# Ten pairs instead of eight beside the preparation of the weights, and the experts two pairs later

## The chip, the core and the metric

The kernel runs on one core of one Trainium2 chip. The metric is the device time of one execution in microseconds (us), the median of several runs. The engines are named as the profile names them: PE is the matrix engine (PEld its loading of weights), DVE the vector engine, ACT the scalar engine that does tanh and exp, POOL the general engine, and SP the engine whose queue issues most of the DMAs. Each engine and each queue works its instructions off in order.

## The reference

Three layers follow each other. B = 4 batches, S = 448 positions, all in float32.

```python
# attention, 12 heads of 64
scores = cap * tanh((q @ k.T) / sqrt(64) / cap)
x = softmax(scores) @ v                        # (4, 448, 768)
# four experts, each a causal attention with one head of 64; a position takes its best two
logits = x @ w_gate
for e in range(4):
    a = causal_softmax((x @ wq[e]) @ (x @ wk[e]).T / sqrt(64))
    out += gate[e] * (a @ (x @ wv[e]) @ wo[e])
# MLP with a gate over the positions
h = gelu(out @ w_in); u, v = halves of h
y = out + (u * (w_sg @ layernorm(v) + b_sg)) @ w_out
```

## The kernel before

**Pairs.** The attention is worked off in 24 pairs of heads, six (HP) for each batch. `slot(i, side)` writes out the program of pair i: the scores of its first half and their tanh and exp on ACT (p), the weighted sum of the values of pair i-1 (po), the scores of the second half, the sums of the exps of every second pair (sum), and the adding up of the exps on DVE (pb; from the second batch on POOL does a part of it). At five places it calls `side(place)`, which puts other work there: "a" twice, beside the halves of the scores, then "w", "p" and "n". Instructions keep this order on PE, DVE, ACT and POOL until the attention ends; after it a planner that simulates the time orders them by itself.

**Preparation.** Beside the first eight pairs (PRE_SLOTS = HP + 2, lines 613 and 625) the side work is `prepare_weights`. The first MLP weight (w_in, stored in 64-bit words) comes in 12 units: `convert(u)` turns one into float32 with seven DVE instructions, `products(u)` multiplies it with wo (PE, w2ps) and at the end of each half `rnd`/`rest` split the product into a high part on ACT and a low part on DVE (w2h, w2l). `turns`, `u_loads` and the expression in line 601 say at which pair a unit is converted, loaded and multiplied. `split_x(k)` splits the experts' weights wqk and wvg, one of six blocks of rows in each of the pairs 2 to 7 (loads by `load_x`).

**Normalising a batch.** After the sixth pair of a batch the sums are inverted on DVE, written to DRAM (rd) and read back over all partitions (rb, `load_rb`); `over_sums` multiplies the attention's output (os) by them and `in_parts` splits it into xh and xl, the experts' inputs. `normed(n, place)` says where: loads at pair 0 of the next batch, place "n"; two products and the first split at pair 1, "n"; the rest within pair 2.

**Experts.** `PLAN` spreads the experts' work of a batch over eleven steps. `planned(n)` (line 491) puts step 0 of batch b at pair 6(b+1)+2: queries and keys (qk, steps 0, 1, 4, 5), values (v, steps 2, 3), scores (a) with their exps (pe) (`weigh`, steps 2, 3, 6, 7), transposes (tr, `turn`) and the weighted values (av, `attend`). What is left after pair 24 comes from `experts_end`, beside the MLP (`mlp_a`, `mlp_b`, `mlp_c`: hv, hu, sp, o).

**Other side work.** `w_out` converts the MLP's last weight in eight pieces through the buffers rb0 and rb1, which `load_rb` uses too: a load (wuw), DVE instructions (wum), three on POOL, and two stores to DRAM (wud). From pair 8 on it takes three pieces in six pairs (lines 518 to 522).

Of the kernel before, what the change touches and what calls it, by code (L numbers as in the profile page):

```python
# [10 lines left out]
F32 = mybir.dt.float32  # L11
# [10 lines left out]
B, H, S, D = 4, 12, 448, 64  # L22
HP = H // 2
DM = H * D
KC = DM // 128
E, HD = 4, 64
# [11 lines left out]
def drain(gen):  # L38
    for _ in gen:
        pass  # L40
# [16 lines left out]
def together(main, side, ratio):  # L57

    yield from interleave(main, side, ratio)
    yield from side  # L60
# [12 lines left out]
def build(ctx: ExitStack, tc: tile.TileContext, a: dict):  # L73
    nc = tc.nc
# [3 lines left out]
    def rnd(eng, out, in_):  # L78

        if eng == "a":  # L80
            act.activation(out, in_, AF.Copy)
        elif eng == "v":
            dve.tensor_copy(out, in_)
        else:
            pool_e.tensor_scalar(out, in_, 1.0, 0.0, op0=ALU.mult, op1=ALU.add)

    def rest(eng, out, in_, hi):

        e = dve if eng == "v" else pool_e
        e.tensor_tensor(out, in_, hi.bitcast(F32), op=ALU.subtract)  # L90
# [127 lines left out]
    def values(b, hp, vv):  # L218
        po = ps_o.tile([128, 512], F32, tag="po", name=f"po{b}_{hp}")
        for c in range(NC):  # L220
            for j in range(2):
                mm(po[64 * j:64 * j + 64, :S], vv[:, j, c, :], pend[b, hp][c // 2][:, j, c % 2, :],
                                 start=(c == 0), stop=(c == NC - 1))
            yield 805.0
        if hp % 2 == 0:
            os_t[b, hp // 2] = ao.tile([128, 2, S], F32, tag="os", name=f"os{b}_{hp}", bufs=4)
        act.activation(os_t[b, hp // 2][:, hp % 2, :], po[:, :S], AF.Copy)

    def sums(b, i):
# [19 lines left out]
    def slot(i, side):  # L249

        if i == 0:
            ld[0] = load_pair(*pairs[0])
            ld[1] = load_pair(*pairs[1])
        if i + 2 < len(pairs):
            qk = [at.tile([128, S], F32, tag=t, name=f"{t}{i + 2}", bufs=3) for t in ("qp", "kp")]
            b, hp = pairs[i + 2]
            nc.sync.dma_start(qk[1], a["kT"][b, :, hp, :])
            nc.sync.dma_start(qk[0], a["qT"][b, :, hp, :])  # L260
            ld[i + 2] = qk
        if i < len(pairs):
            first = scores(*pairs[i], 0, *ld[i][:2])
            drain(islice(first, 2))
            side("a")
            drain(first)
        side("w")
        if i:
            b, hp = pairs[i - 1]
            drain(values(b, hp, ld.pop(i - 1)[2]))  # L270
        if 0 < i < len(pairs) - 1:
            b, hp = pairs[i + 1]
            vv = at.tile([CP, 2, NC, D], F32, tag="vv", name=f"vv{b}_{hp}", bufs=3)
            nc.sync.dma_start(vv, a["v"][b, :, 2 * hp:2 * hp + 2])
            ld[i + 1] = (*ld[i + 1], vv)
        if i < len(pairs):
            side("a")
            drain(scores(*pairs[i], 1, *ld[i][:2]))
        side("p")
        if i:  # L280
            b, hp = pairs[i - 1]
            if hp % 2 == 1:
                drain(sums(b, hp // 2))
        if i < len(pairs):
            add_up(*pairs[i])
        side("n")
# [6 lines left out]
    def load_rb(b, h2):  # L293
        rb = rbs[b, h2] = xp.tile([128, 2, S], F32, tag=f"rb{h2 % 2}", name=f"rb{b}_{h2}")
        for r in range(2):
            nc.sync.dma_start(rb[64 * r:64 * r + 64],
                              rb_d[b][r::2, h2:h2 + 1, :].rearrange("r o s -> o r s").to_broadcast([64, 2, S]))

    def over_sums(b, h2):
        x = os_t[b, h2]  # L300
        dve.tensor_mul(x, x, rbs.pop((b, h2)))
        if h2 == 0:
            load_rb(b, 2)

    def in_parts(b, h2):

# [7 lines left out]
    def normed(n, place):  # L314

        b = (n - 1) // HP - 1
        step = (n % HP, place)
        if n > B * HP + 2:
            return
        if step == (0, "n"):  # L320
            load_rb(n // HP - 1, 0)
            load_rb(n // HP - 1, 1)
        elif b < 0:
            return
        elif step == (1, "n"):
            over_sums(b, 0)
            over_sums(b, 1)
            in_parts(b, 0)
        elif step == (2, "a0"):
            in_parts(b, 1)  # L330
        elif step == (2, "w"):
            over_sums(b, 2)
        elif step == (2, "a1"):
            in_parts(b, 2)

    wu_done = []
# [150 lines left out]
    def planned(n):  # L487

        work = {"a": [], "w": [], "p": [], "t": [], "n": []}
        for b in reversed(range(B)):  # L490
            for place, f, *args in PLAN.get(n - (b + 1) * HP - 2, []):
                work[place].append((b, f, args))
        return work

    def run(works):
        for b, f, args in works:
            w = f(b, *args)
            if w is not None:
                yield from w

    ws = [w_out(k, i) for k in range(4) for i in range(2)]

    def beside(n):

        work = planned(n)
        halves = ["a0", "a1"]

        def side(place):
            if place == "a":
                drain(run(work["a"][:1]))  # L510
                del work["a"][:1]
                normed(n, halves.pop(0))
            elif place == "p":
                drain(together(run(work["p"]), run(work["t"]), 0.3))
            else:
                drain(run(work[place]))
                normed(n, place)
            if place == "n" and n > HP + 1:
                if n % HP in (3, 4, 5) and ws:
                    drain(ws.pop(0))  # L520
                if n % HP in (2, 3, 4) and ws:
                    next(ws[0])
        return side

    def experts_end(n):

        for m in range(n, B * HP + 20):
            work = planned(m)
            for place in ("a0", "w", "a1", "n"):
                normed(m, place)  # L530
            for place in "aw":
                yield from run(work[place])
            yield from together(run(work["p"]), run(work["t"]), 0.3)
            yield from run(work["n"])
            if ws:
                yield from ws.pop(0)


    def prepare_weights(pool):
# [7 lines left out]
            raw[u] = pool.tile([128, FH], I64, name=f"wi{n}_{k}w", tag="w64", bufs=5)  # L547
            nc.sync.dma_start(raw[u], a["w_in"][:, k, n * FH:(n + 1) * FH])

        def load_x(k):  # L550
            for name, w in (("wqk", 2 * E * HD), ("wvg", E * HD + E)):
                t = st[name, k] = pool.tile([128, w], F32, tag=f"st{name}", name=f"{name}{k}", bufs=2)
                nc.sync.dma_start(t, a[name][:, k, :])

        def convert(u):
            m = pool.tile([128, FH], I32, name=f"wi{u}m", tag="m64", bufs=5)
            e = pool.tile([128, FH], I32, name=f"wi{u}e", tag="e64", bufs=2)
            p, e = from64(raw.pop(u), m, e)
            dve.tensor_tensor(p, p, e, op=ALU.add)
            parts[u] = p  # L560

        def split_x(k):
            for name, hi, lo in (("wqk", wqk_h, wqk_l), ("wvg", wvg_h, wvg_l)):
                t = st.pop((name, k))
                rnd("a", hi[:, k, :], t)
                rest("v", lo[:, k, :], t, hi[:, k, :])

        def products(u):
            n, k = units[u]
# [10 lines left out]
                    for o, d in ((oh, w2_d[0]), (ol, w2_d[1])):  # L580
                        nc.sync.dma_start(d[:, m, n * 512:(n + 1) * 512], o.bitcast(F32))

        turns = [(0,), (1, 2), (3, 4), (5, 6), (7, 8), (9, 10), (11,), ()]
        u_loads = [(1, 2, 3), (4, 5), (6, 7), (8, 9), (10, 11), (), (), ()]

        def side(n):
            todo = list(turns[n])

            def at_place(place):
                if place == "a" and todo:  # L590
                    convert(todo.pop(0))
                elif place == "w":
                    for u in u_loads[n]:
                        load(u)
                    if n == 0:
                        nc.sync.dma_start(wt, a["woT"])
                        st["neg"] = constants(pool)
                    if 0 < n <= KC:
                        load_x(n - 1)
                elif place == "p" and n > 1:  # L600
                    for u in (2 * n - 4, 2 * n - 3):
                        products(u)
                elif place == "n":
                    if n == 3:
                        dve.tensor_copy(neg[:, S - CP:], st.pop("neg"))
                    if n > 1:
                        split_x(n - 2)
                if n > 0:
                    normed(n, place)
            return at_place  # L610
        return load, side

    PRE_SLOTS = HP + 2

    xp = ES(tc.tile_pool(name="xp", bufs=1, reuse_waits="tile"))
    with tc.tile_pool(name="pre", bufs=2) as pre:
# [85 lines left out]
    st = {}  # L702
# [184 lines left out]
```

## Time and profile before

| what | value |
|---|---|
| median of 3 runs | 584.55 us (582.46 to 584.84) |
| the profiled execution | 582.48 us, span 580.7 us |
| busy share of the span | PE 93%, DVE 63%, ACT 56%, POOL 25% |
[...]
| DMA | 53.98 MB, mean 93 GB/s |
| chain that ended last | PE 56%, DVE 24%, ACT 8%, DMA 7% of the span |

The span runs from the first to the last instruction; the 1.8 us that the execution takes beyond it lie around it. A share of busy time is a mean over stages with different limits: the chain, which goes back from the last instruction to whatever released each step, has 24% on DVE although PE is busy 93% of the time.

### The profile page before, as it was taken

The page shows a single profiled execution, that of the slowest core. Times are in us where ns is not written, and L with a number is a line of the kernel's source. Part 1 is how long each engine was busy: PE and PEld are TensorE (multiplying, and loading weights), DVE is VectorE, ACT ScalarE, POOL GpSimd, SP SyncE. Part 2 cuts the span into 40 slices and gives each one's busy share as a digit, 9 for nine tenths or more (in the row PEclk, how much of TensorE's full clock was granted, in tenths as well). Part 3 has the DMA queues.
Part 4 walks back from the last instruction along what each step waited for, and adds up shares of the span by engine and source line. Part 5 has one row for each costly group of instructions (what it writes and reads, how often), then busy time and mean ns, then how long its engine had stood idle before and what let it go on. Part 6 is the DMA issues. An engine that isn't in the chain of part 4 may idle for free.

```text
span 580.7 us, 7591 instructions
## 1 busy us (share of the span) xinstructions
PE 540.2 (93%) x2732; PEld 348.1 (60%) x2732; DVE 364.6 (63%) x731; ACT 324.3 (56%) x514; POOL 142.6 (25%) x180
## 2 busy tenths in 40 slices
PE   7999787799899989999989969999999998999997
PEld 2333222455555554554555546778768887989996
DVE  3999997445658456767455469578770589375310
ACT  5988668277777856666857223463553344243211
POOL 0000111033351163431163205327322212031000
PEclk9999999699999999999999986999999999999999
DMA  8966427323326133154011044010601000001111
GB/s 248 333 212 193 135 75 209 97 78 116 108 75 185 50 103 97 35 145 136 17 55 56 28 109 156 21 44 0 216 34 49 16 1 31 33 16 49 49 47 63
DMA packets 28900, 53.98 MB, mean 93 GB/s; under 512 B 3968, under 2 KB 20672, under 8 KB 28864
## 3 DMA queue, kind: packets, MB, share of 16 engines
q1 hardware_dynamic: 27712, 48.26, 27.1%
q0 software_dynamic: 1152, 5.24, 2.5%
q8 instruction: 21, 0.34, 0.3%
q14 instruction: 15, 0.12, 0.1%
HBM read 41.83 MB, written 11.67 MB: 92 GB/s over the span
## 4 chain that ended last, share of the span: by engine, by line
PE 56%; DVE 24%; ACT 8%; DMA 7%; issue 3%; SPq 1%; POOL 1%; DVEq 0%; ACTq 0%; POOLq 0%
PE o L119 15%; PE sp L119 7%; PE qk L119 6%; PE v L119 5%; DVE pb L104 5%; DMA rb<-rd 5%; ACT p L104 5%; PE po L119 4%; PE s L119 4%; PE hu L119 3%; DVE wum L104 3%; PE tr L454 3%; ACT pe L104 2%; PE hv L119 2%; PE a L119 2%
## 5 line engine op out<-in xcount | busy, mean ns | idle before, releaser
L104 ACT ACTIVATE p<-s,tsc 112x896 f32<-112x896 f32 x96 | 91.5, 1007 | 31.4 <-PE s L119 31.4
L119 PE MATMUL s<-qp,kp 64*112 64x448 f32 x384 | 87.6, 557 | 3.9 <-ACT p L104 3.9
L104 ACT ACTIVATE p<-p,capt 112x1792 f32<-112x1792 f32 x48 | 85.9, 1790 | 1.3
L104 POOL TENSOR_TENSOR pb<-p 112x896 f32<-112x896 f32 x18 | 40.2, 2235 | 162.6 <-ACT p L104 155.3
L119 PE MATMUL po<-p,vv 112*64 112x448 f32 x384 | 77.3, 545 | 0.0
L104 DVE TENSOR_TENSOR pb<-pb,p 112x896 f32<-112x896 f32 x48 | 52.1, 1085 | 18.1 <-ACT p L104 17.3
L119 PEld LDWEIGHTS s<-qp,kp 64*112 64x112 f32 x384 | 32.2, 172 | 50.3 <-issue 22.4
L104 ACT ACTIVATE pe<-a,m 112x112 f32<-112x112 f32 (+3 forms) x64 | 31.2, 493 | 51.0 <-DVE m L104 49.6
L119 PE MATMUL qk<-xh,wqk_h 128*128 128x448 f32 x96 | 41.2, 430 | 13.2 <-DVE xh L104 13.2
L119 PEld LDWEIGHTS po<-p,vv 112*64 112x64 f32 x384 | 25.6, 137 | 44.1 <-issue 42.5
L104 POOL TENSOR_SCALAR pe<-pe,cs 112x112 f32<-112x112 f32 (+1 forms) x64 | 35.7, 576 | 50.2 <-DVE cs L104 50.2
L104 DVE CUSTOM_DVE_ANT_0 a<-a,neg 112x112 f32<-112x112 f32 (+3 forms) x64 | 28.0, 464 | 21.3 <-PE a L119 21.2
L119 PE MATMUL a<-qk 64*112 64x224 f32 (+3 forms) x128 | 34.6, 451 | 6.1 <-ACT pe L104 5.8
L119 PE MATMUL qk<-xh,wqk_l 128*128 128x448 f32 x96 | 37.4, 390 | 0.0
L119 PEld LDWEIGHTS qk<-xh,wqk_h 128*128 128x128 f32 x96 | 19.5, 203 | 26.8 <-DVE xh L104 12.5
L119 PE MATMUL o<-gl,wu_h 128*128 128x448 f32 x96 | 35.4, 369 | 0.0
L119 PE MATMUL o<-gh,wu_h 128*128 128x448 f32 x96 | 35.2, 367 | 0.0
L119 PE MATMUL o<-gh,wu_l 128*128 128x448 f32 x96 | 35.0, 368 | 0.0
L104 ACT ACTIVATE ob<-o 128x448 f32<-128x448 f32 x24 | 13.0, 541 | 37.5 <-PE o L119 37.5
L119 PE MATMUL v<-wvg_h,xh 128*112 128x260 f32 x96 | 28.8, 300 | 0.9 <-ACT pe L104 0.9
L119 PEld LDWEIGHTS a<-qk 64*112 64x112 f32 x128 | 13.5, 179 | 26.9 <-ACT pe L104 12.3
L104 DVE COPY pt<-tr 112x112 f32<-112x112 f32 (+3 forms) x32 | 14.0, 448 | 23.9 <-PE tr L454 23.9
(226 smaller groups left out, 1133.6 us busy)
## 6 DMA issues: line engine op xcount, KB each, us to landing
kp<-in_kT_dram SPq DMA_DIRECT2D x24, 224.0 KB, 4.1
qp<-in_qT_dram SPq DMA_DIRECT2D x24, 224.0 KB, 4.2
vv<-in_v_dram SPq DMA_DIRECT2D x24, 224.0 KB, 4.1
rb<-rd SPq DMA_DIRECT2D x24, 224.0 KB, 4.8
out_dram<-ob SPq DMA_DIRECT2D x24, 224.0 KB, 1.9
wuw<-in_w_out_dram SPq DMA_DIRECT2D x8, 384.0 KB, 3.4
wud<-wuw SPq DMA_DIRECT2D x16, 192.0 KB, 1.9
wqk<-in_wqk_dram SPq DMA_DIRECT2D x6, 256.0 KB, 2.9
```

The source lines that it names most:

```text
L104: ins = f(*args, **kw)
L119: pin(nc.tensor.matmul(*args, **kw))
L454: pin(nc.tensor.transpose(g[:CP, j * CP:(j + 1) * CP], pe[:, j * CP:(j + 1) * CP], ident))
```

## The change

The first stage takes ten pairs instead of eight (PRE_SLOTS = HP + 4): `turns`, `u_loads` and the new `u_products` spread the twelve units over them. `load_x` and `split_x` go. `experts_weights(n, place)` takes their place: six parts, cut by columns for wqk (queries and keys of two experts each) and by rows for wvg, loaded at pairs 7 to 12 and split at pairs 8 to 13, the later four beside the experts. The experts' step 0 moves from pair 6(b+1)+2 to pair 6(b+1)+4. `normed` makes two products at pair 2 of the next batch, the third product and the first split at pair 3, the other splits at pair 4; the load of the third rb moves behind both products. The attention's outputs have five buffers instead of four. `slot` calls `side("a")` twice after the last pair too. `w_out` takes two pieces in six pairs, so that two of the eight are left for `experts_end`.

```diff
-            os_t[b, hp // 2] = ao.tile([128, 2, S], F32, tag="os", name=f"os{b}_{hp}", bufs=4)
+            os_t[b, hp // 2] = ao.tile([128, 2, S], F32, tag="os", name=f"os{b}_{hp}", bufs=5)
@@ normed
-        elif step == (1, "n"):
-            over_sums(b, 0)
-            over_sums(b, 1)
+        elif step == (2, "n"):
+            for h2 in range(2):
+                over_sums(b, h2)
+            load_rb(b, 2)
+        elif step == (3, "n"):
             in_parts(b, 0)
-        elif step == (2, "a0"):
+            over_sums(b, 2)
+        elif step == (4, "a0"):
             in_parts(b, 1)
-        elif step == (2, "w"):
-            over_sums(b, 2)
-        elif step == (2, "a1"):
+        elif step == (4, "a1"):
             in_parts(b, 2)
@@ planned
-            for place, f, *args in PLAN.get(n - (b + 1) * HP - 2, []):
+            for place, f, *args in PLAN.get(n - (b + 1) * HP - 4, []):
@@ new
+    def experts_weights(n, place):
+        qk, vg = (wqk_h, wqk_l, a["wqk"]), (wvg_h, wvg_l, a["wvg"])
+        parts = {8: (*qk, 0, KC, 0, 128), 9: (*qk, 0, KC, 256, 384), 10: (*vg, 0, 3, 0, E * HD + E),
+                 11: (*vg, 3, KC, 0, E * HD + E), 12: (*qk, 0, KC, 128, 256), 13: (*qk, 0, KC, 384, 512)}
+        if place == "w" and n + 1 in parts:
+            _, _, d, k0, k1, c0, c1 = parts[n + 1]
+            t = w_raw[n + 1] = at.tile([128, 780], F32, tag="ws", name=f"ws{n}", bufs=2)
...
+            nc.sync.dma_start(t, d[:, k0:k1, c0:c1])
...
+        elif place == "n" and n in parts:
...
+            rnd("a", hi[:, k0:k1, c0:c1], t)
+            rest("v", lo[:, k0:k1, c0:c1], t, hi[:, k0:k1, c0:c1])
@@ beside
-                if n % HP in (3, 4, 5) and ws:
+                if n % HP in (4, 5) and ws:
                     drain(ws.pop(0))
-                if n % HP in (2, 3, 4) and ws:
+                if n % HP in (3, 4) and ws:
                     next(ws[0])
@@ prepare_weights
-        turns = [(0,), (1, 2), (3, 4), (5, 6), (7, 8), (9, 10), (11,), ()]
-        u_loads = [(1, 2, 3), (4, 5), (6, 7), (8, 9), (10, 11), (), (), ()]
+        turns = [(0,), (1,), (2,), (3, 4), (5,), (6, 7), (8,), (9, 10), (11,), ()]
+        u_loads = [(1, 2), (3,), (4, 5), (6, 7), (8,), (9, 10), (11,), (), (), ()]
+        u_products = [(), (), (0,), (1, 2), (3,), (4, 5), (6,), (7, 8), (9,), (10, 11)]
-    PRE_SLOTS = HP + 2
+    PRE_SLOTS = HP + 4
```

## Rows read from the trace of the kernel before

**Rows 1.** Busy time by stretches: us, five engines, granted clock, DMA share, GB/s.
```profile
6.00:90.00 84.00, 75.89 (x316) 26.78 (x316) 77.72 (x123) 67.95 (x69) 4.89 (x2) 1.00 0.63 199
90.00:112.00 22.00, 14.13 (x54) 7.32 (x56) 12.59 (x16) 9.60 (x11) 2.08 (x1) 0.77 0.69 191
325.00:360.00 35.00, 29.46 (x126) 19.62 (x125) 22.29 (x43) 11.34 (x32) 8.59 (x15) 0.80 0.33 89
```

**Rows 2.** Waits of PE up to 112 us: waited for, us in total, times, longest.
```profile
PE qk L119 <- DVE xh L104: 7.9, 3, 4.2
PE w2ps L119 <- DVE w2l L104: 3.0, 1, 3.0
PE s L119 <- ACT p L104: 3.0, 3, 1.7
```

**Rows 3.** A stretch of 4 us, columns as in rows 1.
```profile
348.00:352.00 4.00, 4.00 (x9) 1.79 (x8) 3.05 (x7) 1.26 (x4) 0.00 (x0) 0.50 0.14 21
```

**Rows 4.** The chain of waits, pair 0: start us, us, what.
```profile
6.48 0.96 PE s L119 x4
```

**Rows 5.** Timeline of PE, pair 6 and pair 8's start: start us, us, what.
```profile
67.19 3.23 PE L119 MATMUL po<-p,vv 112*64 112x448 f32 x16
...
70.35 1.76 PE L119 MATMUL s<-qp,kp 64*112 64x448 f32 x8
...
72.04 1.98 PE L119 MATMUL w2ps<-wi8m,wt 128*128 128x512 f32 x4
...
75.67 0.95 PE L119 MATMUL sum<-pb,onehot 112*32 112x448 f32 x4
...
89.81 1.76 PE L119 MATMUL s<-qp,kp 64*112 64x448 f32 x8
```

**Rows 6.** Timeline of PE, pair 9 and pair 10's start.
```profile
112.50 1.76 PE L119 MATMUL s<-qp,kp 64*112 64x448 f32 x8
...
119.04 0.47 PE L119 MATMUL qk<-xh,wqk_h 128*128 128x448 f32 x1
...
122.88 1.76 PE L119 MATMUL s<-qp,kp 64*112 64x448 f32 x8
```

**Rows 7.** Groups of DVE, 6 to 94 us: busy us, mean ns, idle before.
```profile
L104 DVE TENSOR_TENSOR pb<-pb,p 112x896 f32<-112x896 f32 x16 | 17.4, 1084 | 1.7 <-ACT p L104 1.4
...
L104 DVE TENSOR_TENSOR wqk_l<-wqk,wqk_h 128x512 fp32r<-128x512 f32 x6 | 4.1, 685 | 0.0
```

**Rows 8.** Timeline of DVE and POOL, pairs 5 to 7.
```profile
65.93 0.42 DVE L104 TENSOR_SCALAR wi9m<-wi_3w 128x512 int32<-128x512 int32 x1
66.39 0.89 DVE L104 TENSOR_SCALAR wi9m<-wi9m 128x512 f32<-128x512 f32 x2
...
69.83 1.08 DVE L104 TENSOR_TENSOR pb<-p 112x896 f32<-112x896 f32 x1
...
70.38 2.82 POOL L104 TENSOR_TENSOR pb<-p 112x896 f32<-112x896 f32 x1 [68.70 <-ACT p L104]
...
71.29 2.65 DVE L104 TENSOR_SCALAR wi10m<-wi10m 128x512 f32<-128x512 f32 x2
...
93.93 0.42 DVE L104 TENSOR_TENSOR wvg_l<-wvg,wvg_h 128x260 fp32r<-128x260 f32 x1
```

**Rows 9.** Waits of PE from 112 to 325 us.
```profile
PE a L119 <- ACT pe L104: 5.8, 5, 2.4
```

**Rows 10.** Timeline after the last pair, last batch's normalising.
```profile
330.76 0.96 PE L119 MATMUL sum<-pb,onehot 112*32 112x448 f32 x8
...
345.12 0.71 PE L119 MATMUL qk<-xh,wqk_h 128*128 128x448 f32 x1 [4.12 <-DVE xh L104]
...
353.58 1.08 DVE L104 TENSOR_TENSOR xl<-os,xh 128x896 fp32r<-128x896 f32 x1
```

**Rows 11.** Timeline of SP's queue, one piece of w_out.
```profile
299.53 0.33 SPq L344 DMA_DIRECT2D wuw<-in_w_out_dram  x1
310.17 2.47 SPq L351 DMA_DIRECT2D wud<-wuw  x2
```

More of the change, by code (lines that the diff above doesn't have):

```diff
@@ L266, in slot @@
             drain(first)
+        else:
+            side("a")
         side("w")
@@ L275, in slot @@
             ld[i + 1] = (*ld[i + 1], vv)
+        side("a")
         if i < len(pairs):
-            side("a")
             drain(scores(*pairs[i], 1, *ld[i][:2]))
@@ L301, in over_sums @@
         dve.tensor_mul(x, x, rbs.pop((b, h2)))
-        if h2 == 0:
-            load_rb(b, 2)
     def in_parts(b, h2):
@@ L317, in normed @@
         step = (n % HP, place)
-        if n > B * HP + 2:
+        if n > B * HP + 4:
             return
         if step == (0, "n"):
-            load_rb(n // HP - 1, 0)
-            load_rb(n // HP - 1, 1)
+            for h2 in range(2):
+                load_rb(n // HP - 1, h2)
         elif b < 0:
             return
-        elif step == (1, "n"):
-            over_sums(b, 0)
-            over_sums(b, 1)
+        elif step == (2, "n"):
+            for h2 in range(2):
+                over_sums(b, h2)
+            load_rb(b, 2)
+        elif step == (3, "n"):
             in_parts(b, 0)
-        elif step == (2, "a0"):
+            over_sums(b, 2)
+        elif step == (4, "a0"):
             in_parts(b, 1)
-        elif step == (2, "w"):
-            over_sums(b, 2)
-        elif step == (2, "a1"):
+        elif step == (4, "a1"):
             in_parts(b, 2)
@@ L499, in run @@
                 yield from w
+    w_raw = {}
+    def experts_weights(n, place):
[5 more added lines that the diff above has]
+            t = w_raw[n + 1] = at.tile([128, 780], F32, tag="ws", name=f"ws{n}", bufs=2)
+            t = t[:, :(k1 - k0) * (c1 - c0)].rearrange("p (k c) -> p k c", k=k1 - k0)
+            nc.sync.dma_start(t, d[:, k0:k1, c0:c1])
+            w_raw[n + 1] = t
+        elif place == "n" and n in parts:
+            hi, lo, _, k0, k1, c0, c1 = parts[n]
+            t = w_raw.pop(n)
+            rnd("a", hi[:, k0:k1, c0:c1], t)
+            rest("v", lo[:, k0:k1, c0:c1], t, hi[:, k0:k1, c0:c1])
     ws = [w_out(k, i) for k in range(4) for i in range(2)]
@@ L517, in side @@
                 normed(n, place)
+                experts_weights(n, place)
             if place == "n" and n > HP + 1:
-                if n % HP in (3, 4, 5) and ws:
+                if n % HP in (4, 5) and ws:
                     drain(ws.pop(0))
-                if n % HP in (2, 3, 4) and ws:
+                if n % HP in (3, 4) and ws:
                     next(ws[0])
@@ L528, in experts_end @@
             work = planned(m)
-            for place in ("a0", "w", "a1", "n"):
-                normed(m, place)
+            normed(m, "a0")
             for place in "aw":
                 yield from run(work[place])
+            normed(m, "a1")
             yield from together(run(work["p"]), run(work["t"]), 0.3)
             yield from run(work["n"])
+            normed(m, "n")
             if ws:
@@ L548, in load @@
             nc.sync.dma_start(raw[u], a["w_in"][:, k, n * FH:(n + 1) * FH])
[L550 to L553, printed above, removed]
         def convert(u):
@@ L560, in convert @@
             parts[u] = p
[L562 to L566, printed above, removed]
         def products(u):
@@ L597, in at_place @@
                         st["neg"] = constants(pool)
[L598 to L601, printed above, removed]
+                    experts_weights(n, place)
+                elif place == "p":
+                    for u in u_products[n]:
                         products(u)
@@ L605, in at_place @@
                         dve.tensor_copy(neg[:, S - CP:], st.pop("neg"))
-                    if n > 1:
-                        split_x(n - 2)
+                    experts_weights(n, place)
                 if n > 0:
```

## The prediction

> **What bounds the kernel now.** Read first the busy time by stretches [rows 1]. From 6 to 90 us, the pairs 0 to 7, DVE is busy 77.7 of 84 us and PE 75.9, part of it on weights that wait for DVE: here DVE sets the pace. From 90 to 112 us PE stands for 7.9 of 22 us, and from 325 to 360 us for 5.5 of 35; in both the mean granted clock falls, to 0.77 and 0.80. Then the waits of PE [rows 2] name the first of these: 7.9 us for xh, in three waits, the inputs of batch 0's experts. Everywhere else PE has work.
>
> [...]
>
> So the kernel is a sum of PE's work, plus what PE stands and runs slowly in three places: the preparation, the entry of batch 0 into the experts, and that of batch 3.
>
> **The change part by part.** PE's work stays the same, instruction for instruction. What changes is its order.
>
> *First stage and first entry.* Half of a pair's scores costs 72.04 - 70.35 = 1.69 us of PE, the values 70.35 - 67.19 = 3.16, so a pair 6.54; the sums of two pairs 0.95; two units of products 75.67 - 72.04 = 3.63 [rows 5]; one step of queries and keys 122.88 - 119.04 = 3.84 [rows 6]. At 112.50 us [rows 6] PE has pairs 0 to 8 and one such step behind it. After the change it stands at the same step when pair 10 is done, two pairs further: 2 x 6.54 + 0.95 = 14.0 us of work ahead. If pair 9 ends at T, pair 10 ends at T + 6.54 + 3.84 + 0.95 = T + 11.3, and the gain is 14.0 - (T + 11.3 - 112.5) = 115.2 - T.
>
> What is T? By PE: nine pairs without pair 0's values (55.7), ten units (18.2), four sums (3.8), from 6.48 us [rows 4], with the 3.0 us of early waits for ACT [rows 2], bring it to pair 9 at 87.2; pair 9 with two units takes 10.2, so T = 97.4. By DVE: it closes pair 7 at 94.35 [rows 8], when PE had begun pair 8 at 89.81 [rows 5], 4.5 us before. Up to pair 8's adding up the new order has six splits less (6 x (0.685 + 0.42) = 6.6 [rows 7, 8]), the two splits of the second half's product later (1.4, of the same shape as wqk_l's [rows 7]) and one pair's two addings more (2.2 [rows 7]): 88.5 instead of 94.35, with PE again up to 4.5 ahead. So DVE no longer binds on the whole, but it does in single pairs: a conversion takes 69.83 - 65.93 = 3.9 us [rows 8], so pairs 3 and 5 with two of them need 3 x 1.08 + 7.8 = 11.0 on DVE, pair 5 another 1.4, against 10.2 on PE: 3 us together. T = 100, gain 15.2. The low end of T is PE's 97.4 (gain 17.8). The high end is that all ten pairs keep the old pace of (89.81 - 6.48) / 8 = 10.4 [rows 4, 5]: T = 110.6, gain 4.6.
>
> One thing speaks against so early a T. While POOL adds up (70.38, 2.82 us), a pair of DVE instructions that otherwise takes 0.89 takes 2.65 [rows 8]. POOL adds in the pairs from 6 on; there one conversion is left now (unit 11), afterwards four (units 8 to 11, in three pairs). One to three such blocks of 1.76, instead of one, put 0 to 3.5 us on DVE; I take none, as PE's bound lies above. [...]
>
> The wait for xh goes because the sums' way through DRAM (rd, rb) gets two pairs more, some 20 us, before the first product needs it, and the splits another. Next late is then nothing on DVE but PE itself. If that cover failed, the 7.9 us [rows 2] would come back at pair 10 and leave a gain of 7.3, which the range of T still holds.
>
> *Parts of wqk and wvg split beside the experts.* Four of six, each 768 or 780 columns: on DVE about 0.685 x 1.5 = 1.0 us [rows 7], on ACT an estimate of as much. Each is needed one pair later at the earliest. PE has other work beside; the cost is 0 to 4, I take 1. Their loads, 384 KB each on SP's queue between two pairs' loads, are one in a pair, as many bytes as before in fewer DMAs: nothing.
>
> *The weighing of batch 2.* PE waits 5.8 us in five waits for the experts' exps while ACT serves the attention too [rows 9], the longest 2.4. Steps 2 and 3 of batch 2 now fall on pair 24, which has no scores, and behind it: 2 us gained (0 to 2.4).
>
> *The entry of batch 3.* From the last sums (330.76) to the first xh on PE (345.12) are 14.4 us, to the last xl 353.58 + 1.08 are 23.9 [rows 10]. What PE had beside it was one step with transposes. Now steps 3, 4 and 5 of batch 2 stand there: two value chunks and scores of some 6 us (estimated from one qk step plus half), and two steps of 3.84 with transposes of about 1, in all 15 to 16 us. That covers the first xh. It doesn't cover everything: two w_out pieces now come here, through rb0 and rb1, and a piece takes 299.53 to 310.17 + 2.47, and its landing, about 15 us [rows 11]; if one gets rb0 before the third rb, the last xh comes 15 us later, at some 39. Until then PE also has batch 2's steps 6 to 10 (7 us), two thirds of the first qk step (2.6), and the MLP's first part as soon as its weights are there. The standing and slow time of this place is 5.5 + 6 = 11.5 us; the gain lies between all of it and a loss of as much again as the standing (-5.5). I take 5: PE stands once more, shorter.
>
> *The rest costs nothing*: fewer w_out pieces beside the pairs take DVE work away there; the fifth os buffer and the second "a" after the last pair move no instruction onto PE's path.
>
> Sum: 15.2 - 1 + 2 + 5 = 21. Against the profiled execution's 582.48 this gives 561.5; the median of the runs lies 2.1 higher, at 584.55, which gives 563.5. I say 563.
>
> **The rivals.**
> *Only the first half holds:* batch 3's entry stays as dear, because w_out's piece holds the third rb. For it: the buffers are shared, 15 us a piece [rows 11]. Against: 15 us more PE work beside it. 15.2 - 1 + 2 = 16 are left, less up to 2 lost at the end: 569 to 571.
> *It gains everything:* T = 97.4, no cost in the splits, all 11.5 at the end: 17.8 + 2.4 + 11.5 = 32, so 553.
> *The first stage doesn't do what it says:* the blocks by POOL and the alternating pairs keep DVE the limit at 10.4 a pair, gain 4.6 there and 0 at the end: 579.
> *Slower:* both w_out pieces get rb0 before the third rb. The last xh then comes 24 + 30 = 54 us behind the last sums, against some 16 + 7 + 3 = 26 us of PE work: 28 us of standing and 6 at the low clock again, in place of 11.5, a loss of 22 against gains of 16: 590. It decides from a delay of about 27 us on. Against it: the planner behind the last pair places the first MLP's matmuls into such a gap if their weights are in.
>
> **How the numbers follow.** Forecast, 558 to 568 as its own range: 0.57. Only the first half: 0.21. Everything: 0.10. Doesn't do it: 0.06. Slower: 0.06. 555 to 574 leaves out the outer cases, about 0.17. Within 0.5% (2.9 us, what a measurement can tell from no change) falls a part of the last two, 0.04; slower 0.05; faster 0.91.
>
> **What would show it.** Pair 10 begins at about 100 us (before: pair 8 at 89.81) and no wait of PE for xh stands there; the granted clock is 1.00 from 90 to 112. DVE is less than 90% busy up to pair 9. Behind the last pair PE's wait for xh is under 4 us and the clock stays up. Wrong would be: DVE still over 95% busy at pair 8; PE waiting in pairs 12 and 13 for splits; a stand after the last pair with rb behind wud.

## The result, and the profile after

The change makes the kernel slower by 0.8%: 587.76 us median (585.36 to 589.62) against 583.42 (580.93 to 586.47), 18 runs each, ratio 1.0077 [1.0061, 1.0093]. The profiled execution took 585.36 us, 2.9 more than the one of before. The forecast was 563.

First the busy time by stretches, after, with the columns of [rows 1]:

```profile
6.00:90.00 84.00, 80.31 (x348) 27.75 (x348) 76.47 (x111) 71.86 (x65) 7.45 (x3) 1.00 0.70 208
90.00:112.00 22.00, 19.44 (x84) 8.00 (x81) 19.97 (x23) 17.48 (x17) 8.44 (x2) 1.00 0.56 174
120.00:160.00 40.00, 36.19 (x194) 20.55 (x192) 17.94 (x38) 26.14 (x40) 11.26 (x9) 0.91 0.42 127
300.00:320.00 20.00, 15.92 (x78) 9.11 (x74) 13.02 (x35) 3.80 (x14) 7.37 (x11) 0.83 0.19 61
320.00:340.00 20.00, 16.04 (x88) 13.32 (x89) 12.12 (x37) 4.56 (x14) 4.73 (x8) 0.83 0.31 97
340.00:360.00 20.00, 14.48 (x68) 10.06 (x67) 14.21 (x22) 6.41 (x20) 9.46 (x14) 0.74 0.55 160
```

and the last three stretches in the kernel before:

```profile
300.00:320.00 20.00, 19.02 (x123) 11.88 (x123) 10.39 (x26) 12.79 (x20) 4.59 (x4) 1.00 0.19 61
320.00:340.00 20.00, 18.58 (x112) 11.79 (x110) 11.61 (x33) 7.21 (x22) 3.82 (x8) 1.00 0.12 38
340.00:360.00 20.00, 15.88 (x50) 10.04 (x47) 14.97 (x24) 5.11 (x14) 4.76 (x7) 0.66 0.45 117
```

The first two stretches are cured, as forecast: PE is busy 80.3 instead of 75.9 us up to 90, 19.4 instead of 14.1 from 90 to 112, and the clock stays at 1.00. From 300 to 360 PE is busy 46.4 us where it was 53.5, and for 40 us the clock is 0.83 where it was 1.00.

How much that is in PE's work is estimated by a running sum: each matmul counts with its regular distance from start to start at a granted clock of 1.00 (0.21 us for one of the scores, 0.20 for queries and keys, 0.12 for v), and the difference of two kernels at the same time is the **lead** over before, good to about 1 us for the executions that were profiled. They are one each, and lie off the medians: that of the change 2.4 us below its own, those of e2 and e13 2.6 and 3.4 above, that of e11 2.8 below.

```
us            110   120   140   220   300   330   360   550
after        12.3  12.5   7.3   4.7   5.8  -6.9  -5.1  -3.0
e4           12.1  11.3   7.2   0.3   0.4   0.2  -0.4  -1.0
e2           11.9  11.7   6.5   4.2   4.3  -8.0  -7.7  -9.2
e11          12.6  13.0   7.6   4.7   4.8  -8.0  -4.3  -8.3
e13          12.3   9.7   6.6   3.8   4.3  -0.9  -3.1  -4.5
e14          12.6  11.3   6.1   5.1   6.5   0.5  -1.8  -2.8
```

The change wins 12.5 us by 120, loses 5 of them at once, and from 300 to 360 loses 11 more. The first loss, in the timeline of pair 12 (start us, us, what, what ended the idle time before):

```profile
120.75 0.51 POOL L104 TENSOR_SCALAR wuw<-wum 128x384 fp32r<-128x384 f32 x1 [12.84 <-DVE wum L104]
...
123.42 2.10 POOL L104 TENSOR_TENSOR pb<-p 112x896 f32<-112x896 f32 x1
125.56 2.22 DVE L104 TENSOR_TENSOR pb<-pb,p 112x896 f32<-112x896 f32 x2 [4.89 <-POOL pb L104]
127.69 0.96 DVE L104 TENSOR_TENSOR wvg_l<-ws,wvg_h 128x780 fp32r<-128x780 f32 x1
129.08 0.36 DVE L104 TENSOR_SCALAR wum<-wuw 128x384 int32<-128x384 int32 x1 [0.42 <-DMA wuw<-in_w_out_dram]
...
131.72 0.28 DVE L104 CUSTOM_DVE_ANT_0 a<-a,neg 112x112 f32<-112x112 f32 x1
...
132.59 0.44 PE L119 MATMUL a<-qk 64*112 64x224 f32 x1 [2.31 <-ACT pe L104]
...
133.07 3.19 PE L119 MATMUL s<-qp,kp 64*112 64x448 f32 x7
```

POOL does w_out's piece (from 120.75) ahead of its share of the adding up (pb, 123.42). DVE, in order, stands 4.89 us for that, and then has the split of wvg and the next piece (wum) ahead of the first maximum of the experts' scores, at 131.72. PE had written these scores at 126.2. It then stands 2.31 us, and the seven score matmuls behind the stand take 3.19 us where [rows 5] have eight in 1.76.

The second loss, in the waits of PE from 296 to 362 us (waited for, us in total, times, longest), after:

```profile
PE a L119 <- ACT pe L104: 6.9, 3, 5.1
PE tr L455 <- DVE lg L104: 2.7, 1, 2.7
PE v L119 <- ACT pe L104: 2.3, 1, 2.3
PE a L119 <- ACT qk L104: 1.6, 1, 1.6
```

and before:

```profile
PE qk L119 <- DVE xh L104: 4.1, 1, 4.1
PE tr L454 <- POOL pe L104: 0.7, 1, 0.7
```

The wait for xh has gone, as forecast. In its place stand six waits for batch 2's scores, exps, logits (lg) and transposes, 13.5 us. The timeline behind the last pair answers to [rows 10]:

```profile
313.81 0.96 PE L119 MATMUL sum<-pb,onehot 112*32 112x448 f32 x8
...
316.33 2.94 DVE L104 RECIPROCAL rs<-rs 128x448 f32<-128x448 f32 x1
...
319.20 0.49 DVE L104 CUSTOM_DVE_ANT_0 a<-a,neg 112x336 f32<-112x336 f32 x1
319.31 0.34 SPq L242 DMA_DIRECT2D rd<-rs  x1
...
320.46 0.38 PE L119 MATMUL v<-wvg_h,xh 128*112 128x260 f32 x1 [2.27 <-ACT pe L104]
...
321.26 2.54 SPq L298 DMA_DIRECT2D rb<-rd  x4
...
326.81 1.09 DVE L104 TENSOR_TENSOR os<-os,rb 128x896 f32<-128x896 f32 x1 [2.00 <-DMA rb<-rd]
327.82 0.15 DVE L104 COPY lg<-v 112x4 f32<-112x4 f32 x1
...
327.93 0.35 SPq L345 DMA_DIRECT2D wuw<-in_w_out_dram  x1
328.12 0.97 PE L455 MATMUL tr<-ident,pe 112*112 112x112 f32 x4 [2.69 <-DVE lg L104]
...
335.24 2.52 SPq L352 DMA_DIRECT2D wud<-wuw  x2
339.36 1.24 SPq L298 DMA_DIRECT2D rb<-rd  x2
...
344.85 1.09 DVE L104 TENSOR_TENSOR os<-os,rb 128x896 f32<-128x896 f32 x1 [7.14 <-DMA rb<-rd]
345.86 1.69 DVE L104 CAST xh<-os 128x896 fp32r<-128x896 f32 x3
347.46 3.09 DVE L104 TENSOR_TENSOR xl<-os,xh 128x896 fp32r<-128x896 f32 x3
350.47 0.27 DVE L104 CUSTOM_DVE_ANT_0 a<-a,neg 112x112 f32<-112x112 f32 x1
...
351.94 0.71 PE L119 MATMUL a<-qk 64*112 64x224 f32 x1 [5.05 <-ACT pe L104]
```

The last sums are 17 us earlier than before, and batch 3's first qk, at 356.9, is 12 us later: 42.7 us between the two instead of 13.9 (from the last of the eight sums; the prediction's 14.4 counts from the first).

Three of the six waits, 10.0 of the 13.5 us, end only when DVE has worked off something of batch 3's own normalising that stands ahead in its queue. The maximum at 319.20 comes behind the inversion of batch 3's sums (316.33), and PE waits 2.27 us for the exp that follows. The copy of the logits at 327.82, of values that PE had finished at 324.06 + 0.35 = 324.41, comes behind a multiply for which DVE itself stood 2.00 us for rb, and the transposes wait 2.69. The maximum at 350.47 comes behind the whole split into xh and xl, which had waited for the third rb, and PE waits 5.05. This is read from the rows; no run changes DVE's order, so how much it alone costs isn't shown.

### The profile page after: what moved, and what is told of

Read it like the earlier page. It is cut to its first block, busy times and chain, and to the rows that moved or that the text cites. A ratio compares the mean times of both kernels' runs of the same rounds, so it can differ in the third digit from the quotient of the medians.

```text
span 583.6 us, 7567 instructions
## 1 busy us (share of the span) xinstructions
PE 544.5 (93%) x2732; PEld 350.8 (60%) x2732; DVE 364.6 (62%) x725; ACT 323.4 (55%) x508; POOL 144.4 (25%) x180
## 4 chain that ended last, share of the span: by engine, by line
PE 69%; DVE 13%; ACT 8%; DMA 4%; issue 3%; POOL 2%; SPq 0%; POOLq 0%; DVEq 0%; ACTq 0%
PE o L119 15%; PE s L119 9%; PE po L119 7%; PE sp L119 7%; PE qk L119 6%; PE v L119 6%; ACT p L104 5%; PE w2ps L119 3%; DVE pb L104 3%; PE hv L119 3%; PE hu L119 3%; PE av L119 3%; PE a L119 2%; PE tr L455 2%; DVE wum L104 2%
## 5 line engine op out<-in xcount | busy, mean ns | idle before, releaser
L119 PE MATMUL s<-qp,kp 64*112 64x448 f32 x384 | 93.4, 581 | 4.1 <-ACT p L104 4.1
L104 POOL TENSOR_TENSOR pb<-p 112x896 f32<-112x896 f32 x18 | 43.1, 2395 | 156.3 <-ACT p L104 93.9
L119 PE MATMUL po<-p,vv 112*64 112x448 f32 x384 | 79.0, 554 | 0.0
L119 PEld LDWEIGHTS s<-qp,kp 64*112 64x112 f32 x384 | 33.9, 179 | 53.6 <-issue 24.3
L104 DVE TENSOR_TENSOR pb<-pb,p 112x896 f32<-112x896 f32 x48 | 53.8, 1121 | 19.1 <-ACT p L104 13.3
L119 PEld LDWEIGHTS po<-p,vv 112*64 112x64 f32 x384 | 25.8, 138 | 45.7 <-issue 44.1
L119 PE MATMUL a<-qk 64*112 64x112 f32 (+3 forms) x128 | 34.2, 442 | 16.6 <-ACT pe L104 15.0
L104 POOL TENSOR_SCALAR pe<-pe,cs 112x112 f32<-112x112 f32 (+1 forms) x64 | 35.4, 571 | 45.2 <-DVE cs L104 45.1
L119 PE MATMUL qk<-xh,wqk_h 128*128 128x448 f32 x96 | 38.3, 399 | 2.6 <-DVE xh L104 2.6
L104 DVE CUSTOM_DVE_ANT_0 a<-a,neg 112x112 f32<-112x112 f32 (+3 forms) x64 | 27.8, 464 | 14.8 <-PE a L119 14.8
L119 PE MATMUL o<-gl,wu_h 128*128 128x448 f32 x96 | 35.4, 368 | 0.0
L119 PE MATMUL qk<-xh,wqk_l 128*128 128x448 f32 x96 | 35.3, 367 | 0.0
L119 PE MATMUL v<-wvg_h,xh 128*112 128x260 f32 x96 | 30.5, 318 | 2.3 <-ACT pe L104 2.3
L104 DVE COPY pt<-tr 112x112 f32<-112x112 f32 (+3 forms) x32 | 13.9, 448 | 28.4 <-PE tr L455 28.4
L455 PE MATMUL tr<-ident,pe 112*112 112x112 f32 x160 | 24.6, 268 | 5.4 <-DVE lg L104 2.7
```

The source lines that it names most:

```text
L104: ins = f(*args, **kw)
L119: pin(nc.tensor.matmul(*args, **kw))
L455: pin(nc.tensor.transpose(g[:CP, j * CP:(j + 1) * CP], pe[:, j * CP:(j + 1) * CP], ident))
```

## The experiments

All times are medians beside runs of the kernel before on the same chip. Diffs are against the changed kernel unless it is said otherwise.

**e1, e2: w_out's pieces.** e1 goes back to three pieces in six pairs, e2 holds the two last pieces back until batch 3 is normalised.

```diff
 e1
-                if n % HP in (4, 5) and ws:      # and (3, 4) below
+                if n % HP in (3, 4, 5) and ws:   # and (2, 3, 4) below
 e2, experts_end
-            if ws:
+            if ws and m > B * HP + 4:
```

> The changed kernel, with w_out back at three pieces in six pairs, so that none is left behind the last pair. Theory A (the lead of the first stage is lost at the end because batch 2's steps 2 to 5 stand there with no attention beside them, and only in part because a piece of w_out holds the third rb): the wait for the last rb shrinks, 3 to 7 us faster than the changed kernel, 581 to 585. Rival B (w_out's piece alone costs the lead): 10 us or more faster, 577 or less. Rival C (w_out is irrelevant): within 1.5 us of the changed kernel, 586 to 589.

599.02 us, ratio 1.0271 [1.0246, 1.0295]. All three ranges are missed: the third piece adds a fault of its own, so e1 says little about the change. Its load needs rb0, which the third rb now holds a pair longer, and in pairs 16 and 22 (20.5 and 20.2 us instead of 13.7) DVE stands for it:

```profile
188.19 1.08 DVE L104 TENSOR_TENSOR os<-os,rb 128x896 f32<-128x896 f32 x1
189.31 0.33 SPq L345 DMA_DIRECT2D wuw<-in_w_out_dram  x1
...
192.43 0.36 DVE L104 TENSOR_SCALAR wum<-wuw 128x384 int32<-128x384 int32 x1 [3.15 <-DMA wuw<-in_w_out_dram]
```

> The changed kernel, with the two last pieces of w_out kept back until batch 3 is normalised; the pairs are as in the changed kernel. Theory A: 3 to 7 us faster than the changed kernel, like the run with three pieces, 581 to 585. Rival B: 577 or less. If it gains and the run with three pieces does not, the pieces cost as much in the pairs as at the end.

588.95 us, 1.0106 [1.0080, 1.0132]: no gain. The last multiply by rb comes 8.5 us earlier, and the cast of xh then waits for something else, for PE, which still reads xh for batch 2:

```profile
336.39 1.09 DVE L104 TENSOR_TENSOR os<-os,rb 128x896 f32<-128x896 f32 x1 [3.15 <-DMA rb<-rd]
349.19 1.70 DVE L104 CAST xh<-os 128x896 fp32r<-128x896 f32 x3 [5.21 <-PE qk L119]
```

So the piece ahead of the third rb, visible in the changed kernel as the wait of 7.14 us, is not the cause.

**e3, e4: one part alone, and the delay given back.** e3 keeps the old preparation over eight pairs and has only the delay. e4 keeps the ten pairs; batch 0 catches up, and from batch 1 on everything stands where it stood before.

```diff
 e4
+    FIRST = {**PLAN, 0: [], 1: [], 2: PLAN[0] + PLAN[1], 3: PLAN[2], 4: PLAN[3], 5: PLAN[4] + PLAN[5]}
-            for place, f, *args in PLAN.get(n - (b + 1) * HP - 4, []):
+            for place, f, *args in (PLAN if b else FIRST).get(n - (b + 1) * HP - 2, []):
 with the old places in normed for b > 0, three pieces of w_out, parts split at pairs 7 to 12
```

> The kernel before with eight pairs of preparation as they were, and only the experts two pairs later, with the changed normalising. Theory A (the delay itself costs some 12 us at the end and wins back the first entry, some 11): 582 to 588. Rival B (the delay is harmless, w_out is the cause): 570 to 577. PE's waits behind the last pair should look like those of the changed kernel: several of 1 to 3 us for exps, low clock between them.

600.21 us, 1.0293 [1.0268, 1.0318]. It has e1's fault too (pairs 16 and 22: 20.7 and 20.2 us), so its size isn't that of the delay, and both ranges are missed. But last sums to first qk took 40.7 us here as well, and by the lead it loses 8.0 us from 300 to 550 (-10.6 to -18.6), as the change does (5.8 to -3.0, 8.8): the loss at the end comes with the delay alone, with the old preparation and no piece of w_out behind the last pair.

> The ten pairs of preparation stay, but batch 0 catches up: its steps 0 and 1 share pair 10, 2 and 3 follow in pairs 11 and 12, 4 and 5 share pair 13; from batch 1 on everything stands where it stood before the change, and w_out takes three pieces in six pairs. Theory A: the lead of 12 us at 120 us is kept down to the end but for the denser pairs: 570 to 577. Rival D (the lead melts anyway in the pairs with experts, since these are bound by waits and not by PE): 580 to 584.

581.09 us, 0.9956 [0.9933, 0.9979]: a little faster than before, and the best kernel of this study. The lead of 12 melts to 0.3 by 220, since batch 0's first six steps are pressed into pairs 10 to 13, two each into 10 and 13 (19.7, 15.4, 15.4 and 23.2 us). The time is rival D's. But nothing is lost at the end, and batch 2's waits from 296 to 362 us are gone but for small ones; the one for xh is back:

```profile
PE qk L119 <- DVE xh L104: 7.9, 2, 6.6
...
PE a L119 <- ACT pe L104: 0.3, 1, 0.3
```

So the loss from 300 on belongs to the delay of the later batches, not to the preparation.

**e5 to e8: earlier inputs, later pieces, earlier splits.** e5 moves batch 2's last readers of xh to pair 25 and batch 3's split with them. e6 does no piece of w_out before pair 15. e7 splits the six parts in pairs 4 to 9. e8 is all three.

```diff
 e5
+    LAST = {**PLAN, 3: PLAN[3] + PLAN[4][:1] + PLAN[5][:1], 4: PLAN[4][1:], 5: PLAN[5][1:]}   # for batch 2
 e6
-            if place == "n" and n > HP + 1:
+            if n > 2 * HP + 1 and (place, n % HP) in (("n", 4), ("n", 5), ("w", 0)) and n > 15:
 e7
-        parts = {8: ..., 9: ..., 10: ..., 11: ..., 12: ..., 13: ...}
+        parts = {4: ..., 5: ..., 6: ..., 7: ..., 8: ..., 9: ...}
```

> The changed kernel; only behind the last pair batch 2's work is written in another order: the two value chunks and both remaining query and key steps in one go, transposes after, so that batch 2's inputs xh and xl, which have one buffer, come free early, and batch 3 is normalised in one go behind them. Theory E (the lead is lost there because batch 3's split must wait until steps 3, 4 and 5 of batch 2 have read xh, and PE then has nothing left beside the split): from the last sums to batch 3's first qk some 22 to 28 us instead of 43, 6 to 12 us faster than the changed kernel, 575 to 582. Theory A (batch 2's chains without attention beside them are slow wherever they stand): they come later and cost the same, 585 to 589.

592.38 us, 1.0151 [1.0122, 1.0180]: theory A, 3 us beyond its range. The split ends at 347.5 us, only 3 us earlier than in the change (350.6), because PE came to batch 2's queries and keys late, behind waits of 2.3 and 2.8 us; and PE, which then stands 4.9 us for the MLP's first weights, takes it later still, 45.7 us after the last sums.

> The changed kernel with w_out's first two pieces taken out of pairs 10 and 11: none before pair 15, three in each later batch, at the places n of pairs 4 and 5 and w of pair 0, two behind the last pair as in the changed kernel. Theory F (pairs 12 and 13 are long because w_out's work on POOL and DVE stands ahead of the adding up and of the experts' maxima): pair 12 takes 13 to 14 us instead of 17.1, pair 13 14 to 15 instead of 16.5, the whole 3 to 5 us less, 582 to 585. Rival G (the splits beside the experts do it): pair 12 stays at 16 to 17.

602.45 us, 1.0344 [1.0316, 1.0372]. Pair 12 falls from 17.1 to 12.5 us and pair 13 from 16.5 to 14.8: 6.3 us less together, as theory F has it. The whole is slower for a reason of its own, the pieces put at pair 18, which takes 30.3 us instead of 18.6; the longest wait of PE from 112 to 300 us is 9.9 us, for the experts' exps.

> The changed kernel with all six parts of the experts' weights split in pairs 4 to 9. Rival G: pairs 12 and 13 shrink by 3 us or more each, 582 to 584. Theory F: they shrink by 1 us or less each, and pair 10 begins up to 3 us later: 586 to 591.

589.24 us, 1.0102 [1.0077, 1.0128]. Pairs 12 and 13 take 14.2 and 14.0 us, 5.4 less together, nearly what rival G has, but pairs 8 and 10 take 1.5 and 3.2 more, and the time is theory F's. (Pair 10 varies: it took 14.4 to 16.9 us in the profiles of e2, e5, e11, e13 and e14, which change nothing up to there; pairs 12 and 13 together took 31.9 to 33.7.)

> The three edits together. Theories E and F: the gains add, 572 to 579, below the kernel before. If only the first edit gains: 578 to 582; if none does: 587 or more.

607.53 us, 1.0423 [1.0396, 1.0449], with e6's fault in pair 18 (29.5 us).

**e9, e10, e12: gentler ways back.** e9 gives the delay back step by step, e10 does so without a piece of w_out before pair 16, e12 halves it.

```diff
 e9
+    PLANS = [(4, EARLY), (4, EARLY), (2, LAST), (2, PLAN)]   # EARLY: steps 4 and 5 in one pair
 e10, on e9
-                if n % HP in (4, 5) and ws:
+                if n % HP in (4, 5) and n > 15 and ws:
 e12
+    PLANS = [(3, FIRST), (3, PLAN), (3, LAST), (2, PLAN)]    # LAST: steps 4 and 5 in pair 25
```

> The change, but the two pairs of delay are given back one by one: batches 0 and 1 do their steps 4 and 5 in one pair, batch 2 its steps 0 and 1 (pair 22) and 4 and 5 (pair 25), so that from pair 23 on the experts stand where they stood before the change; batch 3 is normalised at its old places. w_out and the split parts as in the change. Theory D (the loss of the change lies behind the last pair, because batch 2's steps 2 to 5 stand there ahead of batch 3's split and cover nothing): last sum to batch 3's first qk 14 to 20 us instead of 42.7, and the clock of the 40 us behind the last sum back over 0.8; the loss in pairs 12 and 13 stays (+6), of the lead of 12 at 110 us 3 to 6 are left at the end: 577 to 581, ratio 0.988 to 0.996. Rival L (wherever the experts' steps meet the dense pairs, the lead is lost, as in e4: the attention's pairs have no room for two steps in one): the doubled pairs 14, 20 and 22 take 3 us more each, and the time is 582 to 587, ratio 0.998 to 1.006.

601.63 us, 1.0307 [1.0267, 1.0346]; last sums to first qk 35.4 us. Both theories miss the time: the lead is gone by 220 and -5.2 at 300, and it goes on falling at the end.

> e9 and no piece of w_out before pair 16 (four beside the pairs from then on, four left for the end). Theory D with the splits and pieces as the cause of pairs 12 and 13: pair 12 near 12.5 us instead of 17.1 and pair 13 below 15; 3 to 5 us faster than e9, so 573 to 577, ratio 0.981 to 0.988, if the four pieces at the end don't delay batch 3's rb. Rival W (the pieces cost the same wherever they stand; with four at the end the rb's of batch 3 or w_h wait for rb0 and rb1): within 2 us of e9 or slower, last sum to first qk of batch 3 over 20 us.

601.35 us, 1.0291 [1.0264, 1.0317]. Pairs 12 and 13 are cured here too (12.5 and 14.8 us, lead 12.3 at 160), and pairs 14 and 16 give it back with 20.5 and 20.4 us. The time is rival W's.

> The change with half the delay: batch 0 begins at pair 10 with steps 0 and 1 in one pair and is from there on one pair later than before the change, as batches 1 and 2 are; batch 2 does steps 4 and 5 together in pair 25, and batch 3 is normalised at its old places. Two pieces of w_out stand beside the preparation (pairs 2 and 4), six in pairs 10, 11, 16, 17, 22, 23, none at the end; the six parts are split in pairs 7 to 12. Theory F (what is late at the end is batch 2's weighing: each of its steps that stands behind the attention's last matmuls costs PE 1 to 3 us of standing and as much at the low clock): only one of its two steps stands there now, so last sum to batch 3's first qk is 16 to 24 us instead of 42.7, the lead of 12 at 110 us falls to 4 to 7 in pairs 10 to 13 and 2 to 5 are left: 578 to 582, ratio 0.991 to 0.997. Rival G (any shift against the old order of the steps costs all of the lead, as e9 shows): no lead at 300 us or over 30 us from last sum to first qk, 585 to 595, ratio 1.003 to 1.02.

599.43 us, 1.0287 [1.0256, 1.0317]; last sums to first qk 32 us. With two pieces beside the preparation pair 6 takes 15.7 us instead of 9.3 (PE waits 4.0 us for w2l), and the lead is -4.6 at 170 already. That is nearer to the rival, 4 us beyond its range; but the pieces beside the preparation are a loss of their own, so what half the delay costs by itself isn't shown. Pairs in which two steps meet are among the long ones throughout: 10 and 13 in e4, 14, 20 and 22 in e9 (18.3, 18.1 and 21.3 us; 13.7, 14.2 and 13.7 in the change), 10 in e12 (20.3).

**e11, e13 to e15: what holds PE behind the last pair.** e11 is e2 with the inputs' buffers free: batch 2's steps 3 to 5 read the weights. e13 makes the maxima and exps of batch 2's first weighing read the queries, so that they no longer hold the scores' PSUM tiles. e14 is both, e15 is e13's edit in the kernel before.

```diff
 e11, on e2
-        xh, xl = X[b]
+        xh, xl = X[b] if (b, ep) != (2, 1) else (wqk_h[:, :, :S], wqk_l[:, :, :S])   # values_chunk: b != 2 or c < 2
 e13
+            x = g[:CP, :n]
+            if (b, ep) == (2, 0):
+                x, g = qk[:CP, 0, :n], pe
-            dve.tensor_tensor_reduce(g[:CP, :n], g[:CP, :n], neg[:, S - n:], -1.0, BIG, ALU.add, ALU.min, m)
+            dve.tensor_tensor_reduce(g[:CP, :n], x, neg[:, S - n:], -1.0, BIG, ALU.add, ALU.min, m)
```

> e2, but batch 2's steps 3 to 5 (two value chunks, the last queries and keys) read the experts' weights wqk in place of the inputs xh and xl: as many instructions of the same shapes, wrong numbers in batch 2, and nothing on PE holds the one pair of input buffers behind the last pair. Theory D' (the split of batch 3 waits for PE, which must read batch 2's inputs first; in e2 the cast of xh stood 5.2 us for that, 13 us after the last multiply by rb): the cast of xh follows the multiplies at once, about 337 us instead of 349; batch 3's first qk comes 24 to 30 us after the last sums instead of 42.9, and the time falls by 4 to 9 us against e2: 580 to 585, ratio 0.995 to 1.002. Rival E (PE stands for the experts' own chains of scores, maxima, exps and transposes of batch 2, not for the inputs; the inputs only come late because PE itself is late): xh is ready early, but PE takes it no earlier than 38 us after the last sums or stands as long elsewhere, and the time stays within 3 us of e2: 586 to 591, ratio 1.004 to 1.013.

593.44 us, 1.0164 [1.0135, 1.0193]. xh is ready at 338 us, but PE takes it at 367.8, and the time is no better than e2's: the rival, 2 us beyond its range. Ahead of it in PE's order stands the MLP, which waits 4.5 us for its first weights. The input buffers are not the cause either.

> The change; in batch 2's first weighing (the scores a of two of its experts) the maxima and exps read the queries instead of the scores' PSUM tiles, so that PE's score matmuls never wait for ACT to have read them (same instructions, wrong numbers for batch 2). Theory F (the waits for these exps, 6.9 + 2.3 us from 296 to 362, and the low clock behind them are the loss behind the last pair): from 296 to 362 PE waits for ACT's exps less than 3 us, the granted clock of 300 to 330 is back over 0.95, the worked-out lead at 330 us is over 0 instead of -6.9, and the time falls by 5 to 10 us against the change: 578 to 583, ratio 0.99 to 1.0. Rival G' (the end of this stage is set by the sums' way through DRAM, the split and the weights w_h that land at 352 us, so PE only stands later): the lead is better at 330 but the same at 360, time within 3 us of the change: 585 to 590, ratio 1.003 to 1.012.

583.29 us, 1.0004 [0.9979, 1.0028]: 0.7% better than the change, between the two ranges, just short of the first. The waits for the exps shrink from 9.2 to 2.7 us, the clock of 300 to 330 is 0.94 instead of 0.79, and the lead at 330 is -0.9 instead of -6.9. Ten us later it is about -6: now the transposes wait, for DVE's copies (pt, 3.9 us) and for POOL's scaling of the exps (pe), which itself waits for DVE, and DVE stood 4.65 us for rb before it:

```profile
328.92 1.09 DVE L104 TENSOR_TENSOR os<-os,rb 128x896 f32<-128x896 f32 x1 [4.65 <-DMA rb<-rd]
...
337.03 2.56 PE L458 MATMUL tr<-ident,pe 112*112 112x112 f32 x10 [5.40 <-POOL pe L104]
```

> e11 with e13's edit: neither the exps of batch 2's first weighing nor the input buffers hold PE or the split. Theory F: as e13, and batch 3's qk or the first hv fills what is left: 574 to 582, ratio 0.982 to 0.997. Rival G': within 3 us of e11, 588 to 596.

587.65 us, 1.0077 [1.0047, 1.0106]: nearer to the rival. With neither of the two holding it, PE stands for the MLP's first weights, which come next in its order:

```profile
340.98 2.05 PE L119 MATMUL hv<-w_h,yh 128*112 128x512 f32 x4 [12.31 <-DMA w_h<-w2d]
```

> Control: e13's edit in the kernel before, where batch 2's first weighing stands in pairs 22 and 23 and PE waits 2.4 us for it at 294. Theory F and rival G' alike: a gain of 0 to 3 us, 580 to 584, ratio 0.995 to 1.0; more than that would mean that the edit itself saves time and e13 must be read against it.

582.18 us, 0.9971 [0.9953, 0.9989]. The edit alone saves 0.3%, so 0.4% of e13's 0.7 are the change's own, hardly more than the intervals can tell from nothing.

## Why the prediction was wrong

**First stage and first entry: right, a little too large.** Pair 9 ends at 99.87 us; 100 was forecast. That it is so near is in part luck: the 3 us that DVE was to cost in pairs 3 and 5 didn't come (both take 10.2, PE's own pace), and what came in their place is mainly pair 8, with 11.0 us for a fifth group of sums and a wait of 0.7 for pb. The lead is 12.5 us against 15.2; the rest is pair 10, 14.4 us instead of the 11.3 of the working, where PE does wait for xh, 2.6 us in two waits:

```profile
94.62 5.53 POOL L104 TENSOR_TENSOR pb<-p 112x896 f32<-112x896 f32 x1 [8.53 <-ACT p L104]
...
96.12 2.08 DVE L104 TENSOR_TENSOR os<-os,rb 128x896 f32<-128x896 f32 x2
...
105.00 2.91 POOL L104 TENSOR_TENSOR pb<-p 112x896 f32<-112x896 f32 x1 [4.85 <-ACT p L104]
...
105.87 2.99 DVE L104 TENSOR_TENSOR os<-os,rb 128x896 f32<-128x896 f32 x1
...
109.45 0.47 PE L119 MATMUL qk<-xh,wqk_h 128*128 128x448 f32 x1 [1.97 <-DVE xh L104]
```

The multiply by rb at 105.87 takes 2.99 us, 1.08 to 1.09 in the later batches: POOL's addition beside it ends at 107.91, and the multiply 0.95 us behind that. The two multiplies at 96.12 take 2.08 together, also beside an addition of POOL's. The forecast had weighed such blocks for the conversions alone and put them at nothing. Pair 9's end came on time; the loss is in pair 10. The mark "DVE less than 90% busy up to pair 9" failed (76.5 of 84 us is 91%), without harm.

**Parts split beside the experts: mis-sized.** Forecast 1 us, 4 at most. Pairs 12 and 13 take 17.1 and 16.5 us where the pairs 10 and 11 of before, with the same steps, took 12.5 and 13.7; pair 14 gives 1.2 of these 7.4 us back. The price was taken as DVE's time for the splits; what it cost was the place in DVE's queue, behind POOL's piece of w_out and ahead of the experts' maxima. e6 and e7 each take one of the two away, and in these pairs each cures most of it (e7 at the price of longer pairs before them). I had named this wait as a mark of being wrong and given it no price.

**The weighing of batch 2: wrong in sign.** Forecast 2 us gained, because pair 24 has no scores. The waits of the scores for exps are 15.0 us over the run after instead of 5.8, 6.9 of them behind 296 (they are part of the next sum). ACT was free there (14.8 of 60 us busy from 300 on), as the step had it; but the exps need DVE's maxima first, and for the longest wait, 5.05 us, DVE had batch 3's split ahead of them.

**The entry of batch 3: the step that failed.** Forecast 5 us gained, bounded by -5.5; measured -10.9 from 300 to 360 by the lead, of which 7.0 are standing (13.56 us instead of 6.52) and the rest the lower clock. No run shows the 6 us of slow time that the forecast's 11.5 for this place holds beside the standing. What the trace of before shows is a clock of 0.50 to 0.52 from 344 to 356 us (the first and last 4 us here, those between in [rows 3]), with PE busy 10.88 of 12 us, and the starts of qk's matmuls 0.37 us apart there and 0.20 apart behind 358:

```profile
344.00:348.00 4.00, 2.88 (x8) 1.62 (x8) 3.57 (x5) 0.00 (x0) 0.00 (x0) 0.52 0.56 95
352.00:356.00 4.00, 4.00 (x9) 2.42 (x10) 4.00 (x8) 2.25 (x6) 0.76 (x2) 0.50 0.02 1
```

```profile
354.50 0.58 PE L119 MATMUL qk<-xh,wqk_h 128*128 128x448 f32 x1
354.87 0.58 PE L119 MATMUL qk<-xh,wqk_l 128*128 128x448 f32 x1
...
358.04 0.36 PE L119 MATMUL qk<-xh,wqk_h 128*128 128x448 f32 x1
358.24 0.37 PE L119 MATMUL qk<-xh,wqk_l 128*128 128x448 f32 x1
```

An estimate from these numbers is 10.88 x (1 - 0.20 / 0.37) = 5.0 us.

The step put "15 to 16 us" of batch 2's steps as cover beside the wait for xh and added them up as PE's work. They are not work that PE can do at any time: scores, maxima, exps, scaling, transposes and values follow each other over four engines. Beside the attention PE has scores and values of the pairs to do meanwhile; behind the last pair it hasn't. And DVE, which the chain needs, is the engine that inverts batch 3's sums, multiplies by rb and splits: the work that was to cover batch 3's entry stands behind that entry in DVE's queue (10.0 of the 13.5 us of waits). The working had the right question, what PE has to do there, and didn't ask whether that work was itself waiting.

That the delay of the later batches brings the loss is shown from two sides: e3 has the delay without the new preparation and loses as much from 300 on, and e4 takes the delay back and loses next to nothing from 220 on. (e4 also leaves no piece of w_out for the end and splits the parts one pair earlier; e2 and e7, which hold those pieces back or split earlier and change nothing else, gain nothing.) Taking single waits away only moves PE's stand: without w_out's piece the split waits for the input buffers (e2), without these PE comes late all the same (e11), without the exps the transposes wait (e13), without both the MLP's weights (e14). How the 10.9 us divide over these links isn't settled, and an order of DVE with batch 2's maxima and copies ahead of batch 3's normalising is the rival that no run tries. e13 less its control gives 0.4% to the first weighing's exps, about 2.6 us.

**The rivals.** The one on the slower side (590, chance 0.06) is nearest in time, but not by its mechanism: one piece, not two, went ahead of the third rb, held it 8.5 us by e2 where 15 had been reckoned, and taking it away gained nothing. The sum of the terms as measured: 12.5 - 5.2 (120 to 140) - 1.5 (to 300) - 10.9 + 2.1 (behind 360) = -3.0, as the profiled executions differ (2.9).

## What to carry to other kernels

Work that is moved behind the end of a long stage is cover only if it doesn't wait for itself (here it did, 13.5 us in six waits): follow its chain over the engines, and look what else stands in their queues, before its PE time is added up. A small piece of side work can cost what stands behind it in its engine's queue, and not its own duration alone (pairs 12 and 13 took 6.3 us less without w_out's pieces ahead, in e6). When a planned order is shifted against what it was laid beside, reckon with the price of giving the shift back: here only doing so in the first batch (e4) undid the loss at the end, and the lead was spent on it.

## What was unexpected of the hardware

Two stands of PE were followed by different clocks, the shorter one by the lower. After (first two rows) PE stands 1.57 us, and the next 4 us have a granted clock of 0.57, with PE busy throughout; before (last two), it stands 2.35 us, and the clock of the next 4 us stays at 1.00:

```profile
296.00:300.00 4.00, 2.43 (x15) 1.32 (x16) 1.78 (x2) 2.48 (x3) 0.00 (x0) 1.00 0.21 82
300.00:304.00 4.00, 4.00 (x13) 1.08 (x10) 3.73 (x12) 0.00 (x0) 3.01 (x6) 0.57 0.00 0
```

```profile
292.00:296.00 4.00, 1.65 (x11) 0.89 (x10) 3.13 (x11) 1.81 (x5) 3.92 (x7) 1.00 0.00 2
296.00:300.00 4.00, 3.56 (x26) 2.55 (x23) 1.16 (x3) 3.97 (x9) 3.57 (x3) 1.00 0.27 98
```

What tells the two apart no run here shows. And an addition of POOL's was longer beside DVE's work, as DVE's multiply at 105.87 was beside POOL's: it took 2.10 us in pair 12, while DVE stood, and 5.53 at 94.62, while DVE did additions, a split and two multiplies up to 98.20. It ends 1.95 us behind them.
